# Score matmuls of two heads interleaved in the two row halves of TensorE, and later queries and keys transposed by DMA, in an attention and gated feed-forward kernel

## The chip, the cores and the metric

One core of one Trainium2 chip. The time is the device time of one execution in microseconds (us); lower is better. The profile is one execution taken by the hardware profiler.

## The reference, cut to what matters

Four sequences of 768 tokens, eight heads of 64. Heads 0, 2 and 6 ("retrieval") see every earlier token; the other five ("streaming") see the first 4 tokens and the last 64. The result, seen as 3072 tokens of 512 features, goes through a gated feed-forward layer.

```python
scores = (1/8) * matmul(q, k^T)                     # 4 x 8 x 768 x 768
keep   = causal                                     # heads 0, 2, 6
keep   = causal & (key < 4 | q_pos - key < 64)      # heads 1, 3, 4, 5, 7
x      = softmax(where(keep, scores, -1e9)) @ v     # -> [3072, 512]
g, val = x @ w_gate, x @ w_val                      # 512 -> 1536
ffn    = (gelu(g) * val) @ w_out                    # 1536 -> 512
out    = x + sigmoid(x @ w_res) * ffn
```

## The kernel before, in words

Work is cut into six chunks of 512 tokens (`CHUNKS`); chunks 1 and 4 take the last two 128-token tiles of one sequence and the first two of the next, the others four tiles of one sequence. A chunk goes through three steps: attention (`attention`), gate and value (`gate_value`, 12 steps of four gate and four value matmuls of 128x512) and output (`output`, per tile four `res` and twelve `ff` matmuls of 128x512). The output step of chunk c and the attention of chunk c+1 are mixed on the engines.

Nothing of this order is written by hand. Every piece of work is a `Task` with an engine, a guessed duration, dependencies, a priority and buffers from small pools; `Graph.schedule` plays the tasks through with the guesses and fixes, per engine, one order. On the chip each engine runs that list in order and waits on semaphores. So a wrong guess becomes a wait.

The parts that the change touches, with the buffers' names in the trace:

- **Loads.** GpSimd (POOL) issues all loads, since they cast to 16 bits: queries and keys into `qks`, values into `va`, weights into `wg`, `wv`, `wr`, `wo`. SyncE (SP) issues only the 24 stores of `otile`. POOL also builds the masks (`m_diag`, `m_causal`, `m_prev`) near the start and, for all chunks but the last, adds `otile<-otile,xtok` before a store.
- **Queries and keys** (`loads`): per head pair (0,1), (2,3), (4,5), (6,7), VectorE (DVE) copies the rows of `qks` into `rp`, TensorE (PE) transposes them by `ident` into a PSUM bank (`qkT`, 8 matmuls for four tiles, 4 for two), ScalarE (ACT) moves the bank into `qkt` (`qkE`; two of chunk 0's banks go through DVE), and DVE makes a copy of the keys with the four first tokens put into every tile (`kts`). Values get such a copy too (`vs`).
- **Scores** (`attention`): a head's query and key rows lie in partitions 0 to 63 or 64 to 127 of `qkt`, so its score matmuls use 64 of the array's rows. The blocks of one head (up to 512 columns, one bank) are one task; then ACT takes the exponential (into `er` for retrieval heads, `es` for streaming), DVE masks, PE multiplies by the values (`av`, into two banks of their own), DVE divides (`rcp`, `norm`).
- **Features**: DVE casts (`x16`), PE transposes (`xT`), DVE copies out (`xE`).
- **PSUM**: two banks for `av`, six for the rest (`P_ps`): at most 3 for scores and transposes ("scr"), at most 4 for the feed-forward ("moe").

Of the kernel before, what the change touches and what calls it, by code (L numbers as in the profile page):

```python
# [4 lines left out]
NHEAD = 8  # L5
# [28 lines left out]

class Task:
    __slots__ = ("eng", "dur", "fn", "deps", "order", "prio", "bufs", "fset", "dma",
                 "ndeps", "users", "ready", "end", "done", "pos", "snap", "waits",
                 "signal", "name", "sem", "seq", "started")

    def __init__(self, eng, dur, fn, deps, prio, bufs=(), fset=None, dma=0.0, order=(), name=""):  # L40
# [10 lines left out]
        self.started = False  # L51
# [49 lines left out]
class Graph:  # L101
# [16 lines left out]
    def schedule(self):  # L118
# [7 lines left out]
        dma_free, fset = 0.0, None  # L126
# [6 lines left out]
        while left:  # L133
# [3 lines left out]
            for e in ENGS:  # L137
# [36 lines left out]
                if t.dma:  # L174
                    st = max(now + dur + 0.8, dma_free)
                    dma_free = st + t.dma
                    t.end = dma_free + 1.6
                else:
                    t.end = now + dur
# [76 lines left out]
    def emit(self):  # L256
        nc = self.nc
        sems = {e: nc.alloc_semaphore(f"cnt_{e}") for e in ENGS}
        val = {}
        for e in ENGS:  # L260
            n = 0
            for t in self.prog[e]:
                if t.dma:
                    t.sem = nc.alloc_semaphore(f"dma_{t.seq}")
                    val[t] = 16
                else:
                    n += 1 if t.signal else 0
                    t.sem = sems[e]
                    val[t] = n

        def run(name, engine):
            for t in self.prog[name]:
                for w in t.waits:
                    engine.wait_ge(w.sem, val[w])
# [49 lines left out]
def build_kernel(nc, q, k, v, w_gate, w_val, w_out, w_res, out):  # L324
# [14 lines left out]
    P_st = Pool(many("qks", 2, [128, 2, NHEAD, 256], FP16))  # L339
    P_rp = Pool(many("rp", 3, [128, 2, 4, 128], FP16))  # L340
    P_v = Pool(many("va", 2, [128, NHEAD, NT, DHEAD + 1], FP16))
    P_vs = Pool(many("vs", 2, [128, NHEAD, NT - 1, DHEAD + 1], FP16))
    P_qkt = Pool(many("qkt", 2, [128, NPAIR, 2, SEQ], FP16))
    P_kts = Pool(many("kts", 2, [128, NPAIR, SEQ - 128], FP16))
# [12 lines left out]
    P_ps = Pool(banks[2:8], caps={"moe": 4, "scr": 3})  # L357
# [39 lines left out]
    def dma(eng, prio, cost, out_ap, in_ap, bufs=(), deps=(), name="ld"):  # L397
        issue = 0.85 if eng == "pool" else 1.2
        return G.add(eng, issue, lambda e: e.dma_start(out_ap(), in_ap), deps, prio, bufs=bufs, dma=cost, name=name)  # L399
# [20 lines left out]
    def batch(b):  # L420
        if b not in batches:
            B_ = B()
            B_.v, B_.vs, B_.qkt, B_.kts = Buf(P_v), Buf(P_vs), Buf(P_qkt), Buf(P_kts)
            B_.vtok, B_.vstok, B_.qktok, B_.kstok, B_.kfix, B_.vfix = {}, {}, {}, {}, {}, {}
# [3 lines left out]
    def loads(c, si, b, a, z):  # L428
# [5 lines left out]
        base = {0: -60, 1: -15}.get(c, 1000 * (c - 2) + 50)  # L434
        groups = ((0, 2), (2, 4), (4, 8)) if c == 0 else ((0, 8),)
        tok = {}
        for gi, (h0, h1) in enumerate(groups):
            for j, src in enumerate((q, k)):
                t = dma("pool", base + 4 * gi + j, (h1 - h0) * 8 * (0.06 if n == 4 else 0.042),
                        (lambda j=j, h0=h0, h1=h1: lambda: at(st)[:, j, h0:h1, 0:n * 64])(),  # L440
# [3 lines left out]
            if b < 2:  # L444
                for h in range(h0, h1):
                    BB.vtok[h, a] = dma("pool", base + 4 * gi + 2, n * 8 * 0.032,
                                        (lambda h=h: lambda: at(BB.v)[:, h, a:z, 0:DHEAD])(),
                                        v[b, h, lo:hi, :].rearrange("(st p) d -> p st d", p=128), bufs=[BB.v])
            elif (0, 0) not in BB.vtok:
                for h0_ in (0, 4):  # L450
                    t = dma("pool", base + 4 + h0_, 24 * 8 * 0.032,
                            (lambda h0_=h0_: lambda: at(BB.v)[:, h0_:h0_ + 4, :, 0:DHEAD].rearrange("p h s d -> p (h s) d"))(),
                            v[b, h0_:h0_ + 4].rearrange("h (st p) d -> p (h st) d", p=128), bufs=[BB.v])
                    for h in range(h0_, h0_ + 4):
                        BB.vtok[h, 0] = t

        for h in range(NHEAD):
            if IS_RETRIEVAL[h]:
                continue
# [345 lines left out]
```

## Time and profile before

| | |
|---|---|
| median of 3 runs | 334.53 us (334.04 to 334.71) |
| profiled execution | 334.3 us, span 332.6 us |
| PE busy | 294.8 us (89%), 2096 matmuls |
| DVE busy | 197.8 us (59%) |
| ACT busy | 178.8 us (54%) |
| POOL busy | 85.7 us (26%) |

The span is what lies between the first and the last instruction; the execution is 1.7 us longer. Matmuls overlap in their pipeline, so "busy" of PE counts more than the work: how far apart the starts of successive matmuls lie tells the cost.

### The profile page before, as it was taken

The numbers are of one execution on the slowest core, as the hardware profiler recorded it, in microseconds if no ns is written. First come the engines' busy times: TensorE is split into PE (matmuls) and PEld (weight loads), VectorE is DVE, ScalarE is ACT, GpSimd is POOL, SyncE is SP. The second block draws the span as 40 slices with busy tenths as digits, with TensorE's granted clock in tenths as the row PEclk, the third lists the DMA queues.
The fourth block names the chain that finished last, engine by engine and source line by source line (L and its number), as shares of the span: only waits on it lengthen the run. The fifth ranks groups of instructions, "written<-read, shape, count | busy, mean of one in ns | idle before, by whom it ended". The sixth has DMA issues, their size and how long they took to land.

```text
span 332.6 us, 5408 instructions
## 1 busy us (share of the span) xinstructions
PE 294.8 (89%) x2096; PEld 151.3 (46%) x2096; DVE 197.8 (59%) x608; ACT 178.8 (54%) x270; POOL 85.7 (26%) x102
## 2 busy tenths in 40 slices
PE   1566799699995999978999989999979999989995
PEld 0344345355452445544445644455534445544442
DVE  1988445958752566884556875349944337744433
ACT  1665035965249267697356673366784377633310
POOL 8999930503402003171001130012030002110000
PEclk9999999959999799999999999999999999999999
DMA  7999999992906001099000073000000000110002
GB/s 80 109 128 206 184 184 171 147 124 19 141 32 65 0 0 66 32 80 121 24 0 34 33 92 69 0 34 32 34 33 32 0 2 32 43 53 2 0 33 95
DMA packets 50633, 21.31 MB, mean 64 GB/s; under 512 B 34224, under 2 KB 47536, under 8 KB 50608
## 3 DMA queue, kind: packets, MB, share of 16 engines
q0 software_dynamic: 47152, 14.68, 42.4%
q1 hardware_dynamic: 3456, 6.29, 5.1%
q8 instruction: 16, 0.26, 0.3%
q14 instruction: 9, 0.07, 0.1%
HBM read 29.36 MB, written 6.29 MB: 107 GB/s over the span
## 4 chain that ended last, share of the span: by engine, by line
PE 76%; DVE 12%; ACT 8%; DMA 1%; issue 1%; POOL 0%; DVEq 0%; POOLq 0%
PE pb L694 37%; PE pb L719 16%; PE pb L557 9%; ACT qkt L500 8%; PE pb L714 6%; PE pb L625 5%; DVE vs L464 2%; DVE rp L480 2%; PE pb L652 2%; PE pb L489 2%; DVE otile L724 1%; DVE kts L509 1%; DVE kts L513 1%; DVE x L646 1%; DMA qks<-in_k_dram 1%; DVE xT L656 1%
## 5 line engine op out<-in xcount | busy, mean ns | idle before, releaser
L700 DVE SCALAR_TENSOR_TENSOR hT<-gact,pb 128x512 f16<-128x512 f16 x72 | 49.4, 687 | 68.1 <-PE pb L694 63.3
L698 ACT ACTIVATE gact<-pb 128x512 f16<-128x512 f32 x72 | 42.7, 599 | 81.4 <-PE pb L694 79.1
L694 PE MATMUL pb<-xT,wg 128*128 128x512 f16 x288 | 75.5, 386 | 4.6 <-DVE xT L656 3.4
L694 PE MATMUL pb<-xT,wv 128*128 128x512 f16 x288 | 75.2, 384 | 0.4 <-ACT qkt L500 0.4
L719 PE MATMUL pb<-wo,hT 128*128 128x512 f16 x288 | 73.6, 380 | 0.0
L728 POOL TENSOR_TENSOR otile<-otile,xtok 128x512 f32<-128x512 f32 x20 | 25.7, 1290 | 157.2 <-DVE otile L724 147.6
L500 ACT ACTIVATE qkt<-pb 128x512 f16<-128x512 f16 (+1 forms) x30 | 43.9, 1576 | 8.5 <-PE pb L489 8.3
L694 PEld LDWEIGHTS pb<-xT,wg 128*128 128x128 f16 x288 | 27.9, 99 | 38.9 <-DVE xT L656 3.4
L565 ACT ACTIVATE er<-pb 128x512 f16<-128x512 f32 (+2 forms) x72 | 35.2, 544 | 19.0 <-PE pb L557 18.8
L694 PEld LDWEIGHTS pb<-xT,wv 128*128 128x128 f16 x288 | 28.3, 99 | 35.2 <-issue 1.7
L565 ACT ACTIVATE es<-pb 128x512 f16<-128x512 f32 (+1 forms) x60 | 31.9, 564 | 18.6 <-PE pb L557 18.3
L557 PE MATMUL pb<-qkt 64*128 64x128 f16 (+3 forms) x276 | 34.1, 258 | 8.5 <-DVE qkt L497 4.2
L719 PEld LDWEIGHTS pb<-wo,hT 128*128 128x128 f16 x288 | 24.3, 98 | 25.2 <-issue 2.4
L399 POOL DMA_DIRECT2D va<-in_v_dram x36 | 29.4, 864 | 17.0 <-PE pb L557 17.0
L557 PEld LDWEIGHTS pb<-qkt 64*128 64x128 f16 x276 | 16.8, 101 | 21.3 <-ACT qkt L500 5.6
L714 PE MATMUL pb<-wr,xT 128*128 128x512 f16 x96 | 25.9, 394 | 0.0
L722 ACT ACTIVATE srs<-pb 128x512 f32<-128x512 f32 x24 | 14.5, 605 | 19.4 <-PE pb L714 15.1
L489 PE MATMUL pb<-ident,rp 128*128 128x128 f16 x192 | 16.0, 235 | 9.0 <-DVE rp L480 9.0
L724 DVE SCALAR_TENSOR_TENSOR otile<-srs,pb 128x512 f32<-128x512 f32 x24 | 16.3, 679 | 12.0 <-PE pb L719 11.2
L635 DVE TENSOR_TENSOR xtok<-pb,rcp 128x256 f32<-128x256 f32 (+1 forms) x64 | 22.0, 351 | 0.4
L632 DVE RECIPROCAL rcp<-pb 128x4 f32<-128x4 f32 (+1 forms) x64 | 10.8, 175 | 13.7 <-PE pb L625 12.6
L480 DVE COPY rp<-qks 128x512 f16<-128x512 f16 (+1 forms) x64 | 16.2, 313 | 4.6 <-DMA qks<-in_k_dram 4.5
(44 smaller groups left out, 294.5 us busy)
## 6 DMA issues: line engine op xcount, KB each, us to landing
out_dram<-otile SPq DMA_DIRECT2D x24, 256.0 KB, 2.0
wg<-in_moe_w_gate_dram POOLq DMA_DIRECT2D x3, 512.0 KB, 10.9
wv<-in_moe_w_val_dram POOLq DMA_DIRECT2D x3, 512.0 KB, 12.1
wo<-in_moe_w_out_dram POOLq DMA_DIRECT2D x4, 384.0 KB, 14.9
qks<-in_q_dram POOLq DMA_DIRECT2D x3, 512.0 KB, 6.1
qks<-in_k_dram POOLq DMA_DIRECT2D x3, 512.0 KB, 8.6
va<-in_v_dram POOLq DMA_DIRECT2D x4, 384.0 KB, 8.9
qks<-in_q_dram POOLq DMA_DIRECT2D x5, 256.0 KB, 4.4
```

The lines of the kernel that those rows point to most:

```text
L399: return G.add(eng, issue, lambda e: e.dma_start(out_ap(), in_ap), deps, prio, bufs=bufs, dma=cost, name=name)
L480: tokr = G.add("dve", c_dve(2 * n * 128, 4, False), (lambda p=p, rp=rp: lambda e: [e.tensor_copy(out=at(rp)[:, j, 0:n, :].rearrange("t i ( ...
L489: r.append(e.transpose(out=at16(scr)[:, (j * n + i) * 128:(j * n + i + 1) * 128], in_=at(rp)[:, j, i, :], identity=ident[:, :]))
L500: e.activation(out=at(BB.qkt)[:, p, :, lo:hi].rearrange("c t (p j) -> c t j p", j=n), in_=at16(scr)[:, 0:2 * n * 128].rearrange("c (t j p) ...
L557: r.append(e.matmul(at(scr)[:, o:o + nq * 128], lhsT=src, rhs=at(BB.qkt)[half:half + 64, p, 0, q0 * 128:(q0 + nq) * 128], start=True, stop ...
L565: (lambda scr=scr, off=off, cols=cols, et=et: lambda e: e.activation(out=at(et)[:, off:off + cols], in_=at(scr)[:, 0:cols], func=AF.Exp, s ...
L694: return lambda e: [e.matmul(at(dst)[:, :], lhsT=w[:, ci, f * 128:(f + 1) * 128], rhs=at(xtbuf)[:, ci, :], start=(ci == 0), stop=(ci == NC ...
L698: ta = G.add("act", c_act(512), (lambda gb=gb, ga=ga: lambda e: e.activation(out=at(ga)[:, :], in_=at(gb)[:, :], func=AF.Gelu))(), [tg], p ...
L700: th = G.add("dve", c_dve(512), (lambda vb=vb, ga=ga, f=f: lambda e: e.scalar_tensor_tensor(out=at(h)[:, f, :], in0=at(ga)[:, :], scalar=0 ...
L714: e.matmul(at(rb)[:, :], lhsT=at(xtbuf)[:, ci, s], rhs=wr[:, ci, :], start=(ci == 0), stop=(ci == NCB - 1))
L719: e.matmul(at(fb)[:, :], lhsT=at(h)[:, fi, s], rhs=wo[:, fi, :], start=(fi == 0), stop=(fi == NF - 1))
L728: t2 = G.add(on, 0.6 if on == "dve" else 1.3, (lambda ot=ot, lt=lt: lambda e: e.tensor_tensor(out=at(ot)[:, :], in0=at(ot)[:, :], in1=at(x ...
```

## The change

The functions that load and attend are written anew. Four things change.

1. **Score pairs.** Heads are paired (0,2), (4,6), (1,3), (5,7), in the order `ORDER`; the two heads of a pair lie in the two partition halves. One task (`scores`) now holds the blocks of both heads, each head with a bank of its own, and alternates between them. Scores of a chunk also wait until step 10 of the gate and value of the chunk before has been issued (`near_end`). "scr" may hold 4 banks instead of 3.
2. **Chunks 0 to 2** (`loads_rows`): no copy into `rp`; PE transposes straight from `qks`, one head at a time, into the upper or lower 64 partitions of the bank. That takes 16 matmuls in place of 8 for four tiles. Keys and queries have a bank each, of 512 columns at most: keys go out through DVE, queries through ACT. The copy out now writes in order and reads PSUM with a stride; before, it was the other way round. Chunk 0 loads heads 0 to 3 and then 4 to 7 (before: 0 and 1, 2 and 3, 4 to 7).
3. **Chunks 3 to 5** (`loads_natural`): queries and keys are loaded by tile, two DMAs of 64 KB written (128x4x64) each for q and k of a tile, 48 DMAs in all, and 24 DMA transposes issued by SP (128x512, 16 bits) write `qkt`. PE, ACT and `rp` have no part in it.
4. **Values** are loaded by tile for all heads (24 DMAs in place of 36), and `vs` and `kts` are made for all heads or several pairs in one DVE instruction.

The planner's guesses for DMAs and some DVE work change too.

```diff
-    P_ps = Pool(banks[2:8], caps={"moe": 4, "scr": 3})
+    P_ps = Pool(banks[2:8], caps={"moe": 4, "scr": 4})
...
+PAIRS = ((0, 2), (4, 6), (1, 3), (5, 7))
+ORDER = (0, 2, 1, 3)
...
+        for p in ORDER:
+            pr = 1000 * c - 550 + p if c else 40 * ORDER.index(p) - 5
+            heads = PAIRS[p]
+            for j, on in ((1, "dve"), (0, "act")):
+                scr = Buf(P_ps, "scr")
+                def tr(e, heads=heads, scr=scr, j=j):
+                    return [e.transpose(out=at16(scr)[64 * x:64 * x + 64, i * 128:(i + 1) * 128],
+                                        in_=at(st)[:, (j * NHEAD + h) * 256 + i * 64:(j * NHEAD + h) * 256 + (i + 1) * 64],
+                                        identity=ident[:, :]) for i in range(n) for x, h in enumerate(heads)]
...
+                def ev(e, p=p, scr=scr, j=j, on=on):
+                    o = at(BB.qkt)[:, j, a:z, p, :].rearrange("c s (p j) -> c s p j", j=n)
+                    i_ = at16(scr)[:, 0:n * 128].rearrange("c (j s p) -> c s p j", j=n, s=n)
+                    return e.tensor_copy(out=o, in_=i_) if on == "dve" else e.activation(out=o, in_=i_, func=AF.Copy)
...
+    def loads_natural(c, si, b, a, z):
+        base = 1000 * (c - 2) + 50
+        for i in range(a, z):
+            for j, src in ((1, k), (0, q)):
+                ds = [dma("pool", base, 1.0,
+                          (lambda sv=sv, o=o: lambda: sv().rearrange("p (o h d) -> p o h d", o=2, h=4)[:, o, :, :])(),
+                          src[b, :, i * 128:(i + 1) * 128, :].rearrange("(h o) p d -> o p h d", o=2)[o], bufs=[st],
+                          grp=("ld", b, i, j)) for o in range(2)]
+                t = G.add("sp", 1.3, (lambda sv=sv, i=i, j=j: lambda e: e.dma_start(
+                    at(BB.qkt)[:, j, i, :, :], sv(), transpose=True))(), ds, base, bufs=[st, BB.qkt], dma=0.6, name="dT")
...
+            mms, pos, cnt = [], [0, 0], [0, 0]
+            while pos[0] < len(seqs[0]) or pos[1] < len(seqs[1]):
+                y = 0 if pos[1] >= len(seqs[1]) or (pos[0] < len(seqs[0]) and cnt[0] <= cnt[1]) else 1
+                m = seqs[y][pos[y]]
+                mms.append(m)
+                pos[y] += 1
+                cnt[y] += m[6]
...
+                half = slice(64 * x, 64 * x + 64)
+                src = at(BB.kts)[half, kt, p, :] if s else at(BB.qkt)[half, 1, kt, p, :]
+                out_.append(e.matmul(at(scr)[:, o:o + nq * 128], lhsT=src, rhs=at(BB.qkt)[half, 0, q0:q0 + nq, p, :],
+                                     start=True, stop=True))
...
+            if f == NF - 2:
+                near_end[c] = tg
...
-            loads(c, si, b, a, z)
+            (loads_rows if c < 3 else loads_natural)(c, si, b, a, z)
```

What the change does to the engines' lists, at the places that matter. A row is the line, the operation, what is written and read, the shape, and how often in a row.

POOL at the very start, before:

```order
L399 DMA qks<-in_q_dram 128x2x256
L367 ISA
L367 AFFINE_SELECT ident<-ident 128x128
L399 DMA qks<-in_k_dram 128x2x256
L399 DMA va<-in_v_dram 128x4x64 x2
L399 DMA qks<-in_q_dram 128x2x256
L399 DMA qks<-in_k_dram 128x2x256
L399 DMA va<-in_v_dram 128x4x64 x2
L399 DMA qks<-in_q_dram 128x4x256
L399 DMA qks<-in_k_dram 128x4x256
L399 DMA va<-in_v_dram 128x4x64 x4
L383 MEMSET m_diag 128x640
```

and now:

```order
L410 DMA qks<-in_q_dram 128x4x256
L378 ISA
L378 AFFINE_SELECT ident<-ident 128x128
L410 DMA qks<-in_k_dram 128x4x256
L410 DMA va<-in_v_dram 128x8x64 x4
L410 DMA qks<-in_q_dram 128x4x256
L410 DMA qks<-in_k_dram 128x4x256
L394 MEMSET m_diag 128x640
```

Fourteen loads stood ahead of the first mask; now there are eight, larger ones.

ACT around the gate and value of chunk 1 (`gact` is the gelu; `qkt` rows are the moves of chunk 2's queries and keys out of PSUM), before:

```order
L698 ACT_TABLE_LOAD
L698 ACTIVATE gact<-pb 128x512 x4
L500 ACTIVATE qkt<-pb 128x2x4x128 x4
L698 ACTIVATE gact<-pb 128x512 x8
L565 ACT_TABLE_LOAD
```

and now:

```order
L735 ACT_TABLE_LOAD
L735 ACTIVATE gact<-pb 128x512
L512 ACTIVATE qkt<-pb 128x4x128 x4
L735 ACTIVATE gact<-pb 128x512 x11
L613 ACT_TABLE_LOAD
```

Four moves of 1024 columns behind the fourth gelu have become four of 512 behind the first; the keys' four stand on DVE.

PE at the beginning of chunk 3's attention (L557 and L602 are scores, L719 and L758 `ff`, L714 and L753 `res`, L625 and L668 `av`), before:

```order
L719 MATMUL pb<-wo,hT 128x512 x3
L557 MATMUL pb<-qkt 128x128 x2
L557 MATMUL pb<-qkt 128x256 x4
L557 MATMUL pb<-qkt 128x128
L714 MATMUL pb<-wr,xT 128x512 x4
L719 MATMUL pb<-wo,hT 128x512 x6
L557 MATMUL pb<-qkt 128x128 x2
L557 MATMUL pb<-qkt,kts 128x128 x2
L719 MATMUL pb<-wo,hT 128x512 x3
```

and now:

```order
L602 MATMUL pb<-qkt 128x128 x8
L602 MATMUL pb<-qkt 128x384 x2
L602 MATMUL pb<-qkt 128x128 x2
L753 MATMUL pb<-wr,xT 128x512 x4
L758 MATMUL pb<-wo,hT 128x512 x6
L602 MATMUL pb<-qkt 128x256
L758 MATMUL pb<-wo,hT 128x512 x6
L668 MATMUL pb<-va,er 128x65 x4
L602 MATMUL pb<-qkt 128x256 x2
```

A group of scores now holds two heads, which alternate (shown merged), and no `ff` of the chunk before is left for the gate and value that follows.

Later on, POOL and SP depend on each other: SP has the four stores of chunk 0, then eight transposes of chunk 3, then two stores of chunk 1, and so on. POOL has 16 loads of chunk 3, six loads of values (which wait until the sequence two before has left `va`), the four additions of chunk 0, and then loads of chunk 4, of which the second eight wait for the eight transposes of chunk 3 to free `qks`; behind them stand the additions of chunk 1.

More of the change, by code (lines that the diff above doesn't have):

```diff
@@ new lines, in key_sinks @@
+    def key_sinks(b, lo, hi, p0, p1, deps, pr):
+        BB = batch(b)
+        if hi <= lo:
+            return
+        cp = G.add("dve", c_dve((hi - lo) * (p1 - p0) * 128, 3, False),
+                   lambda e: e.tensor_copy(out=at(BB.kts)[:, lo:hi, p0:p1, :], in_=at(BB.qkt)[:, 1, lo:hi, p0:p1, :]),
+                   deps, pr, bufs=[BB.qkt, BB.kts], name="ks")
+        fx = G.add("dve", 0.2,
+                   lambda e: e.tensor_copy(
+                       out=at(BB.kts)[:, lo:hi, p0:p1, 0:N_SINK],
+                       in_=at(BB.qkt)[:, 1, 0:1, p0:p1, 0:N_SINK].to_broadcast([128, hi - lo, p1 - p0, N_SINK])),
+                   [cp] + [BB.ktok[p, 0] for p in range(p0, p1)], pr, bufs=[BB.qkt, BB.kts], name="ksf")
+        for i in range(lo, hi):
+            for p in range(p0, p1):
+                BB.kstok[p, i] = fx
```

420 lines of the change are left out of this document (199 added, 221 removed).

## The prediction

> **What bounds the kernel now.** I read the page, then busy time by stretch (cut where each chunk's gate and value begin and end), then the chain of work that ended last.
>
> ```profile
> span 332.6 us, 5408 instructions
> ...
> PE 294.8 (89%) x2096; PEld 151.3 (46%) x2096; DVE 197.8 (59%) x608; ACT 178.8 (54%) x270; POOL 85.7 (26%) x102
> ```
>
> Columns: the stretch, its length, busy time with instruction counts for PE, PEld, DVE, ACT, POOL, granted clock, DMA share, GB/s.
>
> ```profile
> 0.00:37.41 37.41, 18.46 (x169) 12.77 (x170) 27.26 (x67) 16.19 (x23) 36.40 (x57) 1.00 1.10 138
> 37.41:61.94 24.53, 24.20 (x130) 11.49 (x131) 12.50 (x42) 11.22 (x20) 11.79 (x16) 1.00 1.51 165
> 61.94:90.56 28.62, 25.29 (x217) 13.95 (x217) 21.99 (x109) 16.39 (x29) 6.88 (x6) 0.88 1.08 113
> 90.56:121.61 31.05, 27.00 (x141) 12.30 (x140) 13.65 (x44) 16.77 (x18) 2.25 (x3) 0.95 0.20 26
> 121.61:150.70 29.09, 26.34 (x265) 14.52 (x265) 22.38 (x68) 23.22 (x33) 9.88 (x8) 1.00 0.42 56
> 150.70:172.24 21.54, 21.54 (x101) 9.68 (x102) 11.09 (x34) 10.19 (x16) 1.26 (x1) 1.00 0.52 48
> 172.24:196.57 24.33, 22.81 (x228) 13.73 (x229) 18.92 (x62) 17.03 (x31) 5.73 (x5) 1.00 0.14 31
> 196.57:217.94 21.37, 21.37 (x101) 9.67 (x99) 9.63 (x23) 9.34 (x15) 0.00 (x0) 1.00 0.34 53
> 217.94:246.50 28.56, 26.62 (x263) 15.03 (x261) 21.24 (x88) 20.91 (x31) 4.18 (x4) 1.00 0.08 29
> 246.50:267.33 20.83, 20.83 (x97) 9.28 (x98) 8.26 (x14) 10.64 (x15) 2.17 (x2) 1.00 0.07 26
> 267.33:293.84 26.51, 25.60 (x237) 13.36 (x237) 17.17 (x42) 17.36 (x31) 4.22 (x4) 1.00 0.08 31
> ```
>
> Name them A (chunk 0's attention), B (its gate and value), C (attention of chunk 1 beside output of 0), D, E, F, G, H, I, J and K. J is undisturbed: 96 matmuls of 512 columns in 20.83 us, 0.217 us each. D does the same 96 in 31.05. The chain names why:
>
> ```profile
> 98.60 9.29 ACT qkt L500 x4
> ...
> 142.62 4.74 ACT qkt L500 x2
> ...
> 237.50 7.03 ACT qkt L500 x3
> ```
>
> ACT moving queries and keys out of PSUM holds the chain in D, E and I. By shape (count, busy us, mean ns):
>
> ```profile
> L500 ACT ACTIVATE qkt<-pb 128x1024 f16<-128x1024 f16 x14 | 33.0, 2509 | 5.1 <-PE pb L489 5.1
> L500 ACT ACTIVATE qkt<-pb 128x512 f16<-128x512 f16 x16 | 10.9, 759 | 3.3 <-PE pb L489 3.2
> L497 DVE COPY qkt<-pb 128x1024 f16<-128x1024 f16 x2 | 4.9, 2426 | 1.7 <-PE pb L489 1.7
> L480 DVE COPY rp<-qks 128x512 f16<-128x512 f16 x32 | 7.9, 299 | 4.6 <-DMA qks<-in_k_dram 4.5
> ```
>
> **Prices on PE**, from the timeline (start, us, count):
>
> ```profile
> 140.92 0.74 PE L625 MATMUL pb<-va,er 128*128 128x65 f16 x18
> ...
> 143.72 1.06 PE L489 MATMUL pb<-ident,rp 128*128 128x128 f16 x16
> ...
> 278.13 0.40 PE L557 MATMUL pb<-qkt 64*128 64x128 f16 x4
> 278.37 0.22 PE L557 MATMUL pb<-qkt,kts 64*128 64x128 f16 x1
> 278.38 0.23 PE L557 MATMUL pb<-qkt 64*128 64x128 f16 x1
> 278.43 0.22 PE L557 MATMUL pb<-qkt,kts 64*128 64x128 f16 x1
> ...
> 278.70 0.82 PE L719 MATMUL pb<-wo,hT 128*128 128x512 f16 x3
> 279.46 0.40 PE L557 MATMUL pb<-qkt,kts 64*128 64x128 f16 x4
> 279.79 0.82 PE L719 MATMUL pb<-wo,hT 128*128 128x512 f16 x3
> ```
>
> Sixteen transposes in 1.06 us, of which some 0.22 is the last one's tail: 0.056 us per 128 columns. Eighteen `av` in 0.74: 0.032 each. Three `ff` from 278.70 should end their issue at 279.35, but the scores start at 279.46; four scores (0.224) from there should let `ff` start at 279.68, and it starts at 279.79. So each group of scores costs about 0.2 us for turning from 128 rows to 64 and back. And at 278.37 blocks of head 4 and of head 5, by chance neighbours in the list, start 0.01 us apart, while two of one head are 0.06 apart: the two row halves work at the same time.
>
> **Scores.** In 128-column blocks chunk 3 has 3x10 + 5x7 = 65, chunks 1 and 4 have 77, chunks 2 and 5 94. Paired, only the longer head of a pair counts: 34, 42, 52. PE's own work in a stretch, with the order's groups of scores (before 10, 13, 14 in G, I, K and 14 in E; after 9, 11, 12, 12), 16 `xT` (0.90), 16 `res` (3.46), `ff` at 0.216, and 32 transposes (1.79) except in K:
> - G: 3.64 + 2.0 + av 65x0.032 2.08 + 0.90 + 3.46 + 42 ff 9.07 + 1.79 = 22.9, the stretch is 24.33: 1.4 left over. After, with all 48 ff: 1.90 + 1.8 + 2.08 + 0.90 + 3.46 + 10.37 = 20.5.
> - I: 26.5 of 28.56, left over 2.0; after 21.7.
> - K: 25.8 of 26.51, left over 0.7; after 23.1. E: 26.9 of 29.09, 2.2; after 23.1.
>
> What is left over are waits. I keep 2.0, the upper end of the four, although ACT's moves go: a pair's task needs two banks at once, so it waits longer for banks. The nearest rows bound it by 0.7 (K, no moves) and 6.0 (C). So E 25.1 (-4.0), G 22.5 (-1.8), I 23.7 (-4.9), K 25.1 (-1.4). F and H lose the three and four `ff` that spilled into them: -0.7, -0.5.
>
> **D.** Own work 20.83 + 6 ff 1.3 + one `res` and five scores 0.7 + 1.79 = 24.6; 6.4 are lost behind 9.29 us of moves, in part as clock:
>
> ```profile
> 66.00:75.00 9.00, 8.50 (x72) 4.97 (x70) 5.26 (x26) 5.88 (x12) 0.00 (x0) 0.62 0.96 124
> ```
>
> (that is C; D's own row has 0.95, about 3 us at half clock.) After it ACT has four moves of 512 columns and DVE four beside it. Price of one: 0.76 (the 512 row) to 1.25 (half of 2509); the reading is strided now, not the writing, which no row shows. I take 0.76, as 512 columns written with the shorter stride are nearest. Then 3.0 us of ACT, which four "moe" banks nearly cover: 1.5 left. There are 64 transposes of one head: 1.8 if the halves of 64 columns overlap, 3.6 if not; 2.7. D becomes 25.0: -6.0, between -7.5 and -3.
>
> **C.** Own work 22.6, left over 6.0: 3.4 of it is the clock (0.62 over 9 us), the rest waits on `rp`, moves and `vs` at its start. The pairs save 2.0 and 1.0 in groups (12 to 7), six `ff` (1.3) come in: 20.9. The start is freer, but the four additions of chunk 0 stand on POOL behind loads that wait:
>
> ```profile
> POOL va L399 <- PE pb L557: 17.0, 1, 17.0
> ```
>
> That wait stays, now with six loads of values behind it instead of two. I leave 5: 25.9, -2.7 (bounds -5 and +1).
>
> **A and B.** DVE (27.26 busy) and POOL (36.40) set A.
>
> ```profile
> 9.08 3.04 POOL L399 DMA_DIRECT2D va<-in_v_dram x4
> 11.63 4.95 DVE L464 COPY vs<-va 128x260 f16<-128x260 f16 x1
> 12.01 0.76 POOL L383 MEMSET m_diag<- 128x640 f16 x1
> ...
> 16.35 0.84 POOL L399 DMA_DIRECT2D wg<-in_moe_w_gate_dram x1
> ```
>
> A DVE copy stands still from 11.63 until POOL's masks end and the first weight load is issued. The masks now follow eight loads instead of fourteen (0.76 us each by the first row, the larger ones at most twice that): some 3 us earlier. DVE loses eight copies into `rp` (8x0.299 = 2.4) and has four moves of 0.76 in place of two of 2.43 (-1.8). Together 7.2; I take 6, since the first loads are larger, hold 9 and 2.4 as bounds. B: 32 more transposes, 0 to 1.8, and PE starts it cold as before: +1.0.
>
> [...]
>
> **DMA transposes.** No row shows one. The nearest is a store of 256 KB from SP:
>
> ```profile
> out_dram<-otile SPq DMA_DIRECT2D x24, 256.0 KB, 2.0
> ...
> L734 SPq DMA_DIRECT2D out_dram<-otile x24: 332/332/377, 87.6 to 330.1; - x24
> ```
>
> Half the bytes, so 2.0 us each is my price (0.33 at least, the issue alone). They start behind chunk 0's stores, at about 86; chunk 3 wants them at 153. C to F hide them, unless they are as slow as in the second rival. [...]
>
> **Sum.** A -6.0, B +1.0, C -2.7, D -6.0, E -4.0, F -0.7, G -1.8, H -0.5, I -4.9, K -1.4: -27.0. The profiled execution took 334.3 (0.2 under the median): 307.3, say 307.
>
> **Rivals.**
> 1. *Banks or DVE bind the attention stretches.* Two banks per score task of six, or DVE (22.38 of 29.09 in E) slowed by 26 more POOL issues. For it: C's left over of 6. Against: ACT and DVE lose work. With 5.5 instead of 2 in E, G, I and K: +14, 321. If the halves do not overlap in the new lists, 185 blocks of 0.056 more in chunks 1 to 5: +10, 317.
> 2. *Slow transposes, slower than before.* Chunk 4's loads wait on POOL for chunk 3's eight transposes, chunk 1's additions stand behind those loads, and with three `otile`s a chunk's fourth output tile waits until its first is added and stored. With T per transpose: 86 + 8T + eight issues (7) + addition and store (3.3) must be before about 126, three quarters through E. So T over 3.7 us stalls E by 8 us per us, and chunk 4's second eight again. The gain of 27 is gone at T = 3.7 + 27/16 = 5.4; at 6 the time is 345. Against it: the store's 2.0.
> 3. *More than forecast.* Left over 0.7 instead of 2 in four stretches, A at -9: 299 or less.
>
> **How the numbers follow.** Forecast (300 to 314) 0.52; first rival (314 to 326) 0.26; third 0.10; second 0.07; the remaining 0.05 between 326 and 334. The range 296 to 324 leaves out the second and parts of the ends; its bounds are the sum with A, C, D at their ends and the left over at 0.7 or 5. Faster by over 0.2% (what a measurement here can tell) 0.91, within it 0.02, slower 0.07.
>
> **What would show it.** In the profile after: score starts in pairs 0.01 to 0.02 us apart; D near 25 us with ACT `qkt` rows of 512 columns at 0.76; A ending near 31; G, I and K near 22.5, 23.7 and 25; a DMA transpose landing in about 2 us, no PE wait on an `otile` in E. It is wrong if gate and value stretches stay above 22, or PE waits on POOL or SP.

## The result, and the profile after

The changed kernel takes 323.08 us (median of 4 runs, 321.38 to 323.58); the kernel before, on the same chip, 334.28 (334.01 to 334.71). The ratio is 0.9655, with a 95% interval of 0.9616 to 0.9693. It is faster, by 11.2 us, where 27 were forecast: the direction and the range held, the time missed by 16. Times are medians; those of x2, x4, x7, x9 and x12 below leave out one or two slower executions each.

The page of the changed kernel:

```profile
span 321.7 us, 5361 instructions
...
PE 283.0 (88%) x2096; PEld 137.4 (43%) x2096; DVE 177.9 (55%) x474; ACT 141.8 (44%) x256; POOL 106.2 (33%) x128
...
PEclk9999999899999999879999999999579999989999
```

PE lost 11.8 us of busy time, ACT 37, DVE 20. The last row is the clock by slices, in tenths. Its last three dips (8 and 7, 5 and 7, 8) lie behind E, I and K, where the kernel before kept 1.00. Busy time by stretch, cut as before (A to L, and M for the last output):

```profile
0.00:32.87 32.87, 16.45 (x201) 11.27 (x202) 20.87 (x57) 13.40 (x25) 29.61 (x44) 1.00 1.18 152
32.87:57.36 24.49, 24.49 (x160) 11.13 (x160) 11.64 (x31) 9.64 (x21) 5.07 (x7) 1.00 1.72 186
57.36:84.10 26.74, 23.36 (x223) 12.31 (x223) 20.99 (x92) 14.41 (x28) 18.61 (x23) 0.94 1.25 98
84.10:107.07 22.97, 22.97 (x161) 10.95 (x159) 11.66 (x22) 9.73 (x18) 12.84 (x17) 1.00 0.94 114
107.07:135.68 28.61, 24.03 (x242) 12.17 (x242) 20.77 (x50) 17.31 (x31) 10.77 (x11) 0.97 0.48 70
135.68:158.97 23.29, 23.29 (x96) 9.97 (x96) 8.77 (x15) 7.22 (x13) 13.87 (x19) 0.89 1.44 108
158.97:180.71 21.74, 20.88 (x202) 10.65 (x202) 16.86 (x45) 13.58 (x25) 4.62 (x4) 1.00 0.29 65
180.71:201.45 20.74, 20.74 (x96) 9.32 (x96) 8.77 (x13) 7.22 (x13) 0.62 (x1) 1.00 0.09 23
201.45:231.17 29.72, 23.62 (x223) 11.70 (x223) 20.36 (x79) 15.20 (x28) 5.10 (x4) 0.92 0.07 29
231.17:254.50 23.33, 23.33 (x96) 9.98 (x96) 7.57 (x11) 7.22 (x13) 0.00 (x0) 0.89 0.03 10
254.50:281.68 27.18, 23.92 (x242) 12.06 (x242) 15.85 (x42) 17.32 (x31) 5.06 (x4) 0.98 0.10 40
281.68:303.66 21.98, 21.98 (x97) 9.72 (x97) 7.56 (x11) 7.16 (x12) 0.00 (x0) 0.94 0.00 1
```

Read them against the forecast. D fell from 31.05 to 22.97 and G from 24.33 to 21.74, both further than forecast (25.0 and 22.5). E, I and K (28.61, 29.72, 27.18) hardly moved, or grew, and are 11.6 us over the forecast. In I PE is busy for 23.62 of 29.72: PE has less work than before and waits longer. Another 6.0 lie in the gate and value stretches behind them, F, J and L: the same 96 matmuls that take 20.74 in H at clock 1.00 take 23.3 at 0.89. The remaining stretches are 1.5 under the forecast together.

What PE waits for is in the list of waits (total us, count, longest), first of the changed kernel, then of the kernel before:

```profile
PE pb L693 <- DVE x L689: 12.9, 12, 2.5
```
```profile
PE pb L652 <- DVE x L646: 3.1, 5, 1.3
```

The transposes of the finished features wait 12.9 us for VectorE's cast, against 3.1. The end of I, from the timeline (start, us):

```profile
225.91 0.20 PE L668 MATMUL pb<-va,es 128*128 128x65 f16 x1
...
226.64 1.26 POOL L767 TENSOR_TENSOR otile<-otile,xtok 128x512 f32<-128x512 f32 x1 [12.20 <-DVE otile L763]
...
226.80 1.25 DVE L689 CAST x<-xtok 128x256 f16<-128x256 f32 x1
...
228.11 0.39 PE L693 MATMUL pb<-ident,x 128*128 128x128 f16 x2 [2.00 <-DVE x L689]
...
228.92 1.26 POOL L767 TENSOR_TENSOR otile<-otile,xtok 128x512 f32<-128x512 f32 x1 [1.02 <-DVE otile L763]
228.97 1.37 DVE L689 CAST x<-xtok 128x256 f16<-128x256 f32 x1
...
230.39 0.40 PE L693 MATMUL pb<-ident,x 128*128 128x128 f16 x2 [1.89 <-DVE x L689]
...
231.17 1.89 PE L731 MATMUL pb<-xT,wg 128*128 128x512 f16 x4 [0.39 <-DVE xT L697]
```

The same place in the kernel before, where nine `ff` stand behind the last `av`:

```profile
242.56 0.19 PE L625 MATMUL pb<-va,es 128*128 128x65 f16 x1
242.59 2.11 PE L719 MATMUL pb<-wo,hT 128*128 128x512 f16 x9
```

Three things stand in the changed kernel's end. The last `av` is done at 226, and from there PE has nothing but two small groups of transposes: all 48 `ff` of the chunk before had run by then (in the kernel before, six to fifteen were left behind the last `av` in C, E, G, I and K). Two feature blocks follow each other, because heads 5 and 7 complete blocks 2 and 3 together. And both casts take as long as POOL's addition beside them, 1.25 and 1.37 us, where the same cast takes 0.26 to 0.35 with no addition beside it. Then four gate matmuls take 1.89 us instead of the 1.03 they take in D: the clock has dropped to 0.50. It does so as the last `av` end, behind 4.2 us in which PE was busy for 2.29, and stays there until 236.4:

```profile
222.00:226.20 4.20, 2.29 (x23) 1.25 (x21) 4.03 (x22) 1.45 (x2) 0.00 (x0) 1.00 0.00 0
226.20:231.17 4.97, 0.79 (x4) 0.26 (x5) 4.43 (x9) 0.00 (x0) 2.52 (x2) 0.50 0.16 61
```

### The profile page after: what moved, and what is told of

Its sections match the earlier page's. It is cut to its first block, busy times and chain, and to the rows that moved or that the text cites. A ratio compares the mean times of both kernels' runs of the same rounds, so it can differ in the third digit from the quotient of the medians.

```text
span 321.7 us, 5361 instructions
## 1 busy us (share of the span) xinstructions
PE 283.0 (88%) x2096; PEld 137.4 (43%) x2096; DVE 177.9 (55%) x474; ACT 141.8 (44%) x256; POOL 106.2 (33%) x128
## 4 chain that ended last, share of the span: by engine, by line
PE 81%; DVE 13%; DMA 2%; ACT 2%; issue 1%; POOL 0%; POOLq 0%; DVEq 0%
PE pb L731 41%; PE pb L758 19%; PE pb L753 7%; PE pb L602 5%; PE pb L668 4%; DVE x L689 3%; DVE xtok L678 2%; PE pb L504 2%; PE pb L693 2%; DMA qks<-in_k_dram 2%; DVE es L641 1%; DVE xT L697 1%; DVE otile L763 1%; DVE rcp L675 1%; DVE kts L465 1%
## 5 line engine op out<-in xcount | busy, mean ns | idle before, releaser
L731 PE MATMUL pb<-xT,wg 128*128 128x512 f16 x288 | 79.2, 400 | 2.9 <-DVE xT L697 2.9
L731 PE MATMUL pb<-xT,wv 128*128 128x512 f16 x288 | 76.6, 390 | 0.0
L758 PE MATMUL pb<-wo,hT 128*128 128x512 f16 x288 | 73.1, 380 | 0.0
L731 PEld LDWEIGHTS pb<-xT,wv 128*128 128x128 f16 x288 | 29.0, 101 | 36.7 <-issue 5.4
L613 ACT ACTIVATE es<-pb 128x512 f16<-128x512 f32 (+1 forms) x60 | 30.6, 563 | 18.7 <-PE pb L602 17.0
L758 PEld LDWEIGHTS pb<-wo,hT 128*128 128x128 f16 x288 | 24.0, 98 | 24.5 <-issue 2.2
L410 POOL DMA_DIRECT2D qks<-in_q_dram x29 | 23.1, 827 | 16.5 <-PE pb L504 16.1
L410 POOL DMA_DIRECT2D qks<-in_k_dram x29 | 22.9, 812 | 15.6 <-PE pb L504 9.9
L753 PE MATMUL pb<-wr,xT 128*128 128x512 f16 x96 | 25.5, 391 | 0.0
L410 POOL DMA_DIRECT2D va<-in_v_dram x24 | 21.6, 914 | 10.4 <-PE pb L668 10.4
L602 PE MATMUL pb<-qkt 64*128 64x128 f16 (+3 forms) x276 | 22.7, 256 | 2.2 <-DVE qkt L512 1.1
L693 PE MATMUL pb<-ident,x 128*128 128x128 f16 x96 | 11.9, 243 | 12.9 <-DVE x L689 12.9
L668 PE MATMUL pb<-va,er 128*128 128x65 f16 x252 | 14.7, 200 | 4.5 <-DVE er L641 3.5
L675 DVE RECIPROCAL rcp<-pb 128x4 f32<-128x4 f32 (+1 forms) x64 | 10.6, 171 | 13.0 <-PE pb L668 12.2
```

The source lines that it names most:

```text
L602: out_.append(e.matmul(at(scr)[:, o:o + nq * 128], lhsT=src, rhs=at(BB.qkt)[half, 0, q0:q0 + nq, p, :], start=True, stop=True))
L613: tx = G.add("act", c_act(cols), lambda e: e.activation(out=at(et)[:, off:off + cols], in_=at(scr)[:, 0:cols], func=AF.Exp, scale=SM_SCALE ...
L668: r.append(e.matmul(at(av)[:, (i - a) * 65:(i - a) * 65 + 65], lhsT=at(et)[:, pos:pos + 128], rhs=val, start=(i == a and y == 0), stop=(y ...
L731: return lambda e: [e.matmul(at(dst)[:, :], lhsT=w[:, ci, f * 128:(f + 1) * 128], rhs=at(xtbuf)[:, ci, :], start=(ci == 0), stop=(ci == NC ...
L753: e.matmul(at(rb)[:, :], lhsT=at(xtbuf)[:, ci, s], rhs=wr[:, ci, :], start=(ci == 0), stop=(ci == NCB - 1))
L758: e.matmul(at(fb)[:, :], lhsT=at(h)[:, fi, s], rhs=wo[:, fi, :], start=(fi == 0), stop=(fi == NF - 1))
```

## The experiments

Theory: the pairs do save what was forecast on PE; it is lost at the ends of the attentions, where PE runs dry behind VectorE's chain, with its clock falling after it. Rivals: the row halves overlap less than forecast; or the recorded one, pairs waiting for two banks.

Two columns make the runs comparable. "Behind A" is the span of the profiled execution without stretch A, since A varied with one and the same list of instructions (30.1 to 32.9, see the end). "Idle" is the time in C, E, G, I and K in which PE was not busy (length minus PE's column); in x6, x8, x14, x15 and x18 gate and value begin within the attention, so their stretches are cut earlier. "Scores" is PE's own time for them: from each score's start to the next matmul's, at most 0.25 us, so it holds only a part of each turn between 64 and 128 rows (about 0.2 us a group of scores, by the prediction's rows from 278.70 to 279.79). It goes by starts because a matmul's own time is longer: 512 columns are busy for 0.38 us and start 0.216 us apart.

| run | edit | us | behind A | idle | scores |
|---|---|---|---|---|---|
| before | | 334.3 | 295.2 | 10.4 | 35.4 |
| after | | 323.1 | 288.8 | 18.2 | 22.2 |
| x1_seq | heads of a pair listed in turn | 323.6 | 289.5 | 18.1 | 22.3 |
| x2_add64 | POOL adds 64 of 512 columns | 313.9 | 282.7 | 13.3 | 21.0 |
| x3_natural | pairs 0+1, 2+3, 4+5, 6+7 | 312.7 | 277.4 | 11.9 | 24.1 |
| x4_rows | no DMA transposes | 329.3 | 294.3 | 16.9 | 21.6 |
| x5_castact | cast on ACT | 317.0 | 281.8 | 14.2 | 21.8 |
| x6_split | gate and value begun early | 321.2 | | | 22.4 |
| x7_single | one task a head | 307.6 | 273.4 | 4.3 | 32.5 |
| x8_nat_act_split | x3 + x5 + begun early | 299.1 | | | 24.0 |
| x9_outcap | output may hold two banks | 316.5 | 281.9 | 16.9 | 23.3 |
| x10_hold | 12 `ff` behind the last `av` | 316.8 | 283.7 | 13.6 | 22.0 |
| x11_nat_act_outcap | x3 + x5 + x9 | 317.1 | 281.9 | 11.7 | 25.1 |
| x12_single_nat_act | x3 + x5 + x7 | 311.3 | 276.8 | 5.9 | 34.2 |
| x13_scr6 | scores may hold six banks | 317.6 | 283.5 | 16.8 | 22.6 |
| x14_single_nas | x8 with one task a head | 314.0 | | | 34.4 |
| x15_nas_scr6 | x8 + x13 | 306.9 | | | 25.0 |
| x16_last_single | last pair taken apart | 304.9 | 270.9 | 8.4 | 22.7 |
| x17_first_single | the first three taken apart | 308.0 | 273.6 | 6.6 | 29.2 |
| x18_nas_last | x8 + x16 | 307.6 | | | 28.1 |

In x1, x2 and x10 nearly the same list runs as in the changed kernel (x1: other order inside a task; x2: a shorter addition; x10: 12 `ff` moved). In all others the scheduler places the work anew, and the new list has a part in the result.

**x1: does the order within a pair matter?**

```diff
-            mms, pos, cnt = [], [0, 0], [0, 0]
...
-                cnt[y] += m[6]
+            mms = seqs[0] + seqs[1]
```

> Each score task lists its two heads one after the other instead of alternately; nothing else moves. Theory (the alternation works, and what is lost lies at the ends of the attention stretches): the shorter head's blocks no longer run beside the longer head's, 216 blocks of 0.056 us in all, 12.1 us more of PE, of which 9 to 12 reach the end: 332 to 335 us; the ends of the stretches keep their waits. Rival (the halves overlap little, so the missing gain is here): 323 to 326 us.

323.56 us (320.7 to 324.6), and every stretch within 0.3 us of the changed kernel's. The theory missed, though not as the rival has it: scores cost 22.3 us, as little as in alternation. One task of chunk 3 in the list (banks 6 and 2 are the two heads'):

```
L602 MATMUL pb6<-qkt1 128x384
L602 MATMUL pb6<-qkt1 128x128
L602 MATMUL pb2<-qkt1 128x384
L602 MATMUL pb2<-qkt1 128x128
```

In the trace the matmuls of 384, 384, 128 and 128 columns start at 159.860, 159.874, 160.023 and 160.036: the second head's large one starts 0.15 us before the first head's small one, which is ahead of it in the list. Likewise eight blocks of 128 columns, four of one head and then four of the other, in x1 and then (alternating) in the changed kernel:

```profile
165.64 0.41 PE L602 MATMUL pb<-qkt 64*128 64x128 f16 x8
```
```profile
165.07 0.40 PE L602 MATMUL pb<-qkt 64*128 64x128 f16 x8
```

PE fills the free row half from further down the list. What the change gives is that both heads stand next to each other, not that they alternate: in the kernel before 38 scores started within 25 ns of the one before them, now 166, in x1 166 too. That each engine runs its list in order, as said ahead of the prediction, so does not hold for PE across the two row halves.

**x2 and x5: the cast and POOL's addition.** x2 shortens the addition of chunks 0 to 4 (the other 448 columns lack it), x5 moves the cast.

```diff
 x2
-                out=at(ot)[:, :], in0=at(ot)[:, :], in1=at(xbuf)[:, lt, :], op=ALU.add))(),
+                out=at(ot)[:, 0:w_], in0=at(ot)[:, 0:w_], in1=at(xbuf)[:, lt, 0:w_], op=ALU.add))(),
 x5
-        tc_ = G.add("dve", c_dve(n * 128, 1.5, False), lambda e: e.tensor_copy(
+        tc_ = G.add("act", c_act(n * 128), lambda e: e.activation(func=AF.Copy,
```

> POOL's addition of the output tiles of chunks 0 to 4 takes 64 of 512 columns (the rest of the sum is left out); every queue keeps its order. Theory (a VectorE cast that meets POOL's addition stands still until it ends): the casts of 1.2 to 1.4 us at the ends of E, I and K fall to 0.27 to 0.43, E -0.8, I -2.0, K -0.8, and the gate and value behind them start warmer, -2 to -5: 315 to 319 us. Rival (pairs wait for two banks, or DVE's own work binds): casts stay or the freed time becomes a wait elsewhere, 322 to 324 us.

> The cast of the token tile before it is transposed runs on ACT instead of VectorE; the rest is the changed kernel, planned anew. Theory (a cast on VectorE stands still while POOL adds): the ends of E, I and K have a cast of about 0.6 us on ACT instead of 1.2 to 1.4 and the gate and value behind them start warmer, as with the addition cut to 64 columns: 313 to 318 us. Rival (what counted there was DVE's or POOL's work as such, or ACT's queue becomes the wait): 321 to 326 us.

The theory holds for the ends: 313.9 (6.2 us less behind A; below its range, as A was 2.8 us shorter in the profiled execution) and 317.0 (7.1 less). Its other half does not hold: F, J and L together lose only 0.7 us in x2 and 0.8 in x5, so the attentions become shorter, but gate and value start hardly warmer. The end of I in x2, timeline:

```profile
220.08 0.32 POOL L767 TENSOR_TENSOR otile<-otile,xtok 128x64 f32<-128x64 f32 x1 [13.20 <-DVE otile L763]
220.23 0.31 DVE L689 CAST x<-xtok 128x256 f16<-128x256 f32 x1
...
221.42 0.32 POOL L767 TENSOR_TENSOR otile<-otile,xtok 128x64 f32<-128x64 f32 x1 [1.02 <-DVE otile L763]
221.46 0.42 DVE L689 CAST x<-xtok 128x256 f16<-128x256 f32 x1
```

With additions of 0.32 us the casts take 0.31 and 0.42: the 1.25 and 1.37 were standing still. Not every cast beside an addition does: in C of the changed kernel one takes 0.27 us (at 82.80) beside an addition of 1.45, and what decides is not shown. The first rival feared POOL's loads for DVE; at the ends its additions count. In E the cast at 131.13 takes 0.43 us beside loads, the one at 133.28 takes 1.21 beside an addition. A copy of keys (`kts`, 384 columns) stands between the two and takes 1.22 us while POOL issues two loads; a copy of the same size in D (at 93.94) takes 0.28 beside two others, so what loads cost such a copy is not settled.

**x10 and x6: PE dry and cold.**

```diff
 x10: the last output tile's ff also wait for the last av of the next attention
+        if h == PAIRS[ORDER[-1]][1]:
+            for t in held.get(c - 1, []):
+                t.order.append(prev_t)
 x6: for f < 2
+            for lo, hi in (((0, 2), (2, 4)) if f < 2 else ((0, NCB),)):
+                xt = [t for t in xttoks if t.pos < hi]
```

> The last output tile's twelve `ff` (2.6 us) of each chunk are put behind the last `av` of the next chunk's attention; nothing else is changed by hand, and pairs keep their banks. Theory (the chain of the last pair takes its time either way, and the cold clock comes from PE's idle end): the gate and value stretches F, J and L come back to 20.8, -6.6, the attention stretches keep their length less what `ff` delayed: 312 to 317 us. Rival (the clock falls for another reason, or the `ff` only come on top): 321 to 330 us.

> The first two gate and the first two value tiles of a chunk begin with feature blocks 0 and 1, which need only the first two pairs, and add blocks 2 and 3 when these come; eight matmuls of 0.217 us, 1.7 us, can so run while PE waits for the last pair. Pairs, casts and additions stay. Theory (PE runs dry at the ends of E, I and K, and its clock falls for it): F, J and L lose their cold start, -2.6, -2.7 and -1.3, and 1.2 to 1.7 us of each wait is filled: 311 to 316 us. Rival (the ends are bound by the chain through DVE, and the clock falls for another reason): 319 to 324 us.

x10: 316.8. Its stretches E, F, I, J, K and L:

```profile
104.66:133.73 29.07, 25.52 (x243) 12.70 (x242) 19.07 (x50) 17.32 (x31) 10.88 (x12) 0.94 0.56 74
133.73:154.46 20.73, 20.73 (x96) 9.28 (x96) 9.09 (x15) 7.22 (x13) 13.71 (x18) 1.00 1.58 116
...
197.61:226.99 29.38, 26.63 (x224) 12.80 (x224) 18.73 (x78) 15.19 (x28) 3.84 (x3) 0.88 0.07 28
226.99:247.71 20.72, 20.72 (x97) 9.31 (x95) 8.25 (x12) 7.21 (x13) 1.27 (x1) 1.00 0.04 13
247.71:275.68 27.97, 25.42 (x242) 12.68 (x242) 14.65 (x41) 17.32 (x31) 3.79 (x3) 0.94 0.08 29
275.68:296.42 20.74, 20.74 (x98) 9.42 (x98) 8.25 (x12) 7.16 (x12) 1.27 (x1) 1.00 0.04 13
```

F, J and L lose 2.56, 2.61 and 1.24 us, 6.4 of the 6.6 expected, and E, I and K together grow by 0.9: with work at PE's end, gate and value start warm. The clock still falls, but earlier: it is 0.94, 0.88 and 0.94 in E, I and K, and the `ff` at the end of I run at half speed, nine in 4.03 us instead of 2.11:

```profile
221.82 4.03 PE L761 MATMUL pb<-wo,hT 128*128 128x512 f16 x9
```

So the cold time is not gone; the `ff` take it while the chain runs, and a part of the lower idle time (13.6) is only their slowness. The length of E, I and K does not come from PE: with twelve `ff` put at their ends they stay as long, so their chain sets them. x6 missed (321.2 for 311 to 316, within the rival's 319 to 324): the eight early matmuls are soon done, blocks 2 and 3 are as late as ever, and PE waits inside gate and value instead; its F, from the first early matmul on, is 29.73 us long with PE busy for 25.36.

**x3: which heads end together.**

```diff
-PAIRS = ((0, 2), (4, 6), (1, 3), (5, 7))
-ORDER = (0, 2, 1, 3)
+PAIRS = ((0, 1), (2, 3), (4, 5), (6, 7))
+ORDER = (0, 1, 2, 3)
```

> Pairs are heads 0+1, 2+3, 4+5, 6+7, so each pair completes one feature block and one instead of two is left for the end. Three more blocks of 128 columns stand in a chunk's longer heads, 0.2 to 0.4 us a chunk, and 4 instead of 3 pairs of keys get their sinks on DVE. Theory (two feature blocks at the end are part of what was lost): E -1.5, I -2, K -1, and less cold gate and value, in all 315 to 320 us. Rival (banks bind, the last pair's wait is the same for one block): 323 to 328 us.

312.7, better than the theory's 315 to 320: I falls by 5.5 us to 24.19, and one block less at the end, with the new list, outweighs 1.9 us more for scores.

**x7, x16 and x17: one task a head.**

```diff
-            for r in range(max(len(S_.packs) for S_ in side)):
-                scores(c, BB, p, pr, [(x, S_) for x, S_ in enumerate(side) if r < len(S_.packs)], r)
+            for one in ([[0], [1]] if p == ORDER[-1] else [[0, 1]]):      # x16; x17: !=; x7: always
+                for r in range(max(len(side[x].packs) for x in one)):
+                    scores(c, BB, p, pr, [(x, side[x]) for x in one if r < len(side[x].packs)], r)
```

> Each head's scores are tasks of their own with one bank, as before the change, in the new layouts; one head's tasks follow the other's. Theory (the gain of the pairs is that the two heads' blocks stand side by side, whatever their order; with other work between them each block costs 0.056 us again and each more group 0.2): +3 to +9, 326 to 332 us. Rival (a pair waits for two banks at once, and that is the missing gain): 315 to 321 us.

> Only the last pair of an attention (heads 5 and 7) is scored as two tasks of one head; the other three pairs stay as in the changed kernel. Theory A (two heads that end together make the end: after the last score two exponentials, two masks, two `av` and two feature blocks follow each other): E, I and K lose 2 to 3 us each, and part of the cold starts goes: 311 to 316 us. Theory B (pairs delay the attention all along, the last one no more than the others): 319 to 323 us.

> The other way round: the first three pairs are scored one head at a time, the last pair stays one task. Theory A: the end of each attention stays as it was, and PE pays some 7 us more for scores: 320 to 328 us. Theory B: 308 to 314 us, most of the way to one task a head everywhere.

x7 gives 307.6: PE pays 10.3 us more for scores and the kernel is 15 faster. PE's idle time in the five attentions falls from 18.2 to 4.3 us, and no gate and value starts cold. The theory (326 to 332) missed by 18 us and the rival (315 to 321) by 7: I had taken the price of the halves for the price of the pairs. x16 takes only the last pair apart: 304.9, below the 311 to 316 of theory A, with the scores as cheap as before (22.7). E, F, I, J, K and L of x16:

```profile
103.51:127.68 24.17, 23.22 (x242) 12.07 (x242) 16.97 (x48) 17.25 (x31) 7.91 (x9) 1.00 0.48 64
127.68:148.41 20.73, 20.73 (x96) 9.31 (x96) 12.26 (x18) 7.21 (x13) 16.99 (x22) 1.00 1.63 140
190.20:216.43 26.23, 22.67 (x223) 11.51 (x222) 17.97 (x79) 15.14 (x28) 5.08 (x4) 0.98 0.11 41
216.43:238.27 21.84, 21.84 (x96) 9.57 (x96) 7.56 (x11) 7.22 (x13) 0.00 (x0) 0.95 0.00 1
238.27:262.44 24.17, 23.23 (x243) 12.07 (x242) 14.69 (x42) 17.14 (x31) 3.17 (x3) 1.00 0.06 23
262.44:283.17 20.73, 20.73 (x96) 9.39 (x97) 8.10 (x12) 7.16 (x12) 1.88 (x2) 1.00 0.07 26
```

E is 24.17 and K 24.17, under the 25.1 that was forecast for the changed kernel. In E the last score starts 1.2 us earlier, the last `av` 2.7 us earlier (20.86 instead of 23.53 us into the attention), nine `ff` stand behind it, and DVE is busy for 16.97 instead of 20.77 us: its casts no longer stand behind POOL. That speaks for theory A: the pair that ends together costs much. But x17, the opposite, gives 308.0, the lower edge of theory B, where A wanted 320 to 328: 15.2 us less behind A, nearly the 17.9 of x16. Its lists too leave 9 to 18 `ff` behind the last `av`, except in chunk 4, where there are none. The shares of "ends together" and "delayed all along" are not settled, because every such edit moves the whole list. And one head a task also needs one bank where a pair needs two; these runs don't part that either.

**x9 and x13: banks.**

```diff
 x9
+    P_ps = Pool(banks[2:8], caps={"moe": 4, "scr": 4, "out": 2})      # rb and fb are of kind "out"
 x13
+    P_ps = Pool(banks[2:8], caps={"moe": 4, "scr": 6})
```

> Pairs stay one task with two banks; the output's tiles may hold two of the six banks at a time instead of four. Theory from the run with one task a head (a pair's task, which needs two banks at once, is put behind output tiles that need one, so the output's work is used up before the last pair and nothing is left beside its chain): the scores of E, I and K end earlier, some 12 `ff` stand behind the last `av`, and no gate and value starts cold: 305 to 312 us. Rival (two heads that end together lengthen the chain, whatever the banks do): 317 to 322 us.

> Scores and feature transposes may hold all six banks instead of four, so three pairs' tasks can be under way; nothing else is changed by hand. Theory (a pair waits for two banks at once): the pairs come earlier, E, I and K lose 1.5 to 3 us each and some `ff` stand behind the last pair: 313 to 318 us. Rival (the pace of the exponentials and VectorE's chain set the end, not banks): 320 to 324 us.

316.5 (two executions) and 317.6: 6.9 and 5.3 us less behind A. x13 is in the theory's range; x9 missed it, just under the rival's. Idle time hardly falls in either (16.9 and 16.8 of 18.2); in x9 nearly all of the gain is clock (F, J and L lose 6.4 us together), in x13 a good half (3.2). By these lists banks are a part of the missing 16 us, and not the larger.

**x4: what the DMA transposes are worth.** All chunks use `loads_rows` again.

> Chunks 3 to 5 are loaded by rows and transposed on PE again, as chunks 0 to 2; the DMA transposes are gone. Theory (the transposes cost PE what they cost in B and D, 2.1 to 3.0 us a chunk, in the gate and value stretches, which PE fills): F, H and J +2 to +3 each, 329 to 332 us. Rival (the DMA transposes, SP's 1.3 us for each issue or POOL's more loads are what hurt): 318 to 323 us.

329.3, in the theory's range; 5.5 us more behind A, where 6 to 9 were expected. That is the worth of loading by tile and transposing by DMA together. The scheduler put the transposes of chunks 3 and 4 into the attentions E and G (32.00 and 24.19 us), not into gate and value. SP's eight transposes in D of the changed kernel, and the median from issue to landing:

```profile
87.06 10.64 SPq L534 DMA_TRANSPOSE qkt<-qks x8
```
```profile
qkt<-qks SPq DMA_TRANSPOSE x24, 3.5
```

Each takes 1.3 us of issue, on a queue that has nothing else to do then, and 3.5 us (2.4 to 7.3) to land where 2.0 were forecast; with the eight issued in 10.6 us one behind the other they are done long before chunk 3 wants them. POOL waits for the transposes once, for 5.7 us, PE for an output tile never, so the second rival's stall does not come.

**x8, x11, x12, x14, x15, x18: put together.**

> Three edits together: pairs of neighbouring heads, the cast on ACT, and the first gate and value tiles begun with feature blocks 0 to 2. Theory (one late block, no collision and a filled end take away most of the 17.7 us that E to L have over the forecast): every gate and value stretch near 20.8, E near 26, I near 23.5, K near 25: 301 to 307 us. Rival (the three take away the same few us): 310 to 314 us, as with the pairs of neighbouring heads alone.

> Pairs of neighbouring heads, the cast on ACT, and two banks for the output's tiles. Theory: the halves' saving of 11 to 13 us of PE is kept (about 24 us for all scores), the ends are filled, no cold gate and value: 293 to 300 us. Rival (ACT with scores, casts and moves or the two banks of the output become the wait): 302 to 308 us.

> One score task a head, neighbouring heads in a pair of rows, the cast on ACT. Theory: the ends stay filled as with one task a head alone, the collision with POOL is gone, but scores cost PE some 31 to 33 us instead of 22: 300 to 306 us, slower than the kernel with pairs and two banks for the output. Rival (the halves' saving is not needed, since the chain decides): at or under that kernel's time, 293 to 300 us.

> The fastest kernel so far (pairs of neighbouring heads, cast on ACT, gate and value begun early) with one score task a head: the ends stay filled, the two heads' blocks no longer stand side by side. Theory (the halves' saving of some 8 to 10 us of PE counts once PE is what binds): 304 to 309 us against 299. Rival (one task a head is better in itself, as the step from 323 to 308 us suggests): 290 to 298 us.

> The fastest kernel so far with six instead of four banks for scores. Theory (banks delay the pairs): 294 to 298 us. Rival (PE, filled to 92% of the span, or the exponentials bind, not banks): 298 to 302 us.

> The fastest kernel so far (299 us) with its last pair (heads 6 and 7) scored as two tasks. Theory A: its ends are filled already, so little is left: 296 to 300 us. Theory B: the same. Over 301 us would mean that the planner's new list costs more than the end gains.

x8 (neighbouring heads, the cast on ACT, gate and value begun early) is the fastest: 299.1, 2 us under the theory's range, ratio to before 0.8927 (0.8879 to 0.8975), 24 us under the changed kernel. x14 takes its pairs apart and is 15 us slower, with 10.4 us more for scores; in the changed kernel x7 gained 15 by the same edit. That fits ends that are filled in x8 and not in the changed kernel, so that PE's savings count in the one and not in the other. It is not shown: 15 is more than the 10.4, and x18, which takes apart only the last pair, loses 8.5 with 4.1 more for scores. x11, x12, x15 and x18 add or swap what had helped alone and end at 307 to 317. x11, x12, x14 and x15 lie outside what either side gave them, and x18 beyond the 301 that was to mean a dearer list: these gains do not add, and the list that the scheduler makes of an edit moves the time by as much as the edit itself.

## Why the prediction was wrong

Right: the work on PE. By its blocks and groups scores were to save 1.9 us in G, 2.4 in I, 2.8 each in E and K and 3.0 in C, 12.9 without A, of which 2.4 are turns; by the column "scores", which holds only a part of the turns, they saved 10.3 without A and 13.2 in the whole kernel (35.4 to 22.2). D was to fall to 25.0 and fell to 22.97: its 64 transposes of one head make it only 2.2 us longer than H, 0.035 us each. The two of a pair start 0.003 us apart and the next pair mostly 0.053 later, so their column halves overlap (near the 1.8 of the two bounds); nothing is left of the 1.5 us of waiting, and the moves priced at 0.76 take 0.60 on ACT and 0.68 on DVE:

```profile
L512 ACT ACTIVATE qkt<-pb 128x512 f16<-128x512 f16 x8 | 4.3, 600 | 7.3 <-PE pb L504 7.3
L512 DVE COPY qkt<-pb 128x512 f16<-128x512 f16 x8 | 5.2, 684 | 8.4 <-PE pb L504 8.4
```

B (24.49 for 25.5; its first four gate matmuls take 1.86 us, before 1.87) and C (26.74 for 25.9) came near, G and H as well. A was 32.87 for 31.4, within its own scatter. Rival 2 (slow transposes) is refuted (its 345 us at 6 us a transpose come to 344 by its own terms).

Wrong: the step "What is left over are waits. I keep 2.0, the upper end of the four". By the same sums of PE's work it was 5.5 in E, 1.2 in G, 8.0 in I and 4.1 in K: 18.8 instead of 8.0, 10.8 us. (The largest of the four was 2.2.) The step took the waits of the kernel before as a constant of the stretch and the stretch as PE's own work. In the changed kernel the chain of the last heads through ACT, VectorE and PE sets E, I and K (x10), so the 2 to 3 us of PE work taken out of each become idle time. And that chain had become longer: from the start of the last score to that of the last `av` it takes 5.3 us instead of 1.9 in E, 7.9 instead of 5.9 in I and 5.3 instead of 2.6 in K, and behind it come two blocks at once (x3, x16) and casts that stand still (x2, x5). How the 10.8 us divide among these is open. The sum also let F, J and L run at 20.83 to 20.90; they took 6.0 more, the price of the clock that falls at that thin end (x9 and x10 win it back), and no term stood for it. Together these are 16.8 us where 16 are missing; the other stretches come out 0.7 lower in all.

The first rival had the place right (more left over in the attentions), at a chance of 0.26. That its 321 us are so near the measured 323 is in part luck: it put 14 us more into E, G, I and K, where 10.8 came, with G below the forecast, and had no term for the 6.0 of clock. It named banks and DVE; x13 gives banks 5.3 us behind A, x2 the casts that stand still 6.2, beside POOL's additions and not its loads (93 where 67 were; what those cost on DVE in all is not shown). The mark set for failure, gate and value above 22, is what the profile shows in F and J.

## What to carry to other kernels

When work is taken off the busiest engine, ask at each place where its list ends in a chain through other engines what still covers that chain: here the scores took 13 us less of PE, and against it stood 8 us more of idle time in the attentions and 6 us of cold clock. Look there at how many results end together and at what else holds the engine that has to finish them; taking the last pair apart was worth 18 us, though taking the other three apart was worth 15, so a new list has its own share. Price apart what a change brings together (here neighbourhood and alternation).

## What the runs showed of the hardware

- PE takes matmuls of the idle row half ahead of earlier ones of the other half in its list: in x1 384, 384, 128, 128 columns started, from 159.860 to 160.036, where the list has 384, 128, 384, 128; x1 lost nothing by it (323.56 us beside 323.08).
- POOL issues all 93 loads (67 before), each with its cast to 16 bits. No run puts one on another engine, so whether the cast asks for POOL is not shown.
- The same list of chunk 0 took 30.1 to 32.9 us in different executions. In the long ones (the changed kernel, x1) a VectorE copy of 16 columns takes 1.85 us; in x2 the same copy takes 0.60. POOL makes its masks beside it in both; what decides is not shown:

```profile
11.50 1.85 DVE L468 COPY kts<-qkt 128x16 f16<-128x16 f16 x1
```
```profile
10.31 0.60 DVE L468 COPY kts<-qkt 128x16 f16<-128x16 f16 x1
```

- The clock fell to half behind thin work, before PE was wholly idle: in I behind 4.2 us with PE busy for 2.29, in E behind 3.4 us (130.6 to 134.0) with 0.40. It stayed there until 236.4 and 140.8; the gate matmuls start 0.43 us apart, and F and J cost 2.6 us more than H.
- ACT moves 512 columns out of PSUM with a strided read in 0.60 us; with the strided write of the kernel before, 512 columns took 0.76 and 1024 took 2.51.
